# First x tile loaded in halves, the eighth transposed by DMA, and one group of half rows for the last four output tiles

## The chip, the core and the metric

The kernel runs on one core of a Trainium2 chip. The core has five engines that work side by side and wait for each other through semaphores: TensorE (PE; its weight loads are listed apart, as PEld), VectorE (DVE), ScalarE (ACT), GpSimd (POOL) and SyncE (SP), which only issues transfers. ScalarE and GpSimd issue transfers too. Each engine takes its instructions in the order in which they were queued. The metric is the device time of one execution in microseconds (us), the median of several executions.

## The reference

A block with a linear-attention part and a SwiGLU part is run forward, and the gradient with respect to its input and its weights is returned along with the output. There are 2048 rows of 640 columns, in bfloat16.

```
def _layernorm(x, axis=-1, eps=1e-5):
    m = jnp.mean(x, axis=axis, keepdims=True)
    v = jnp.var(x, axis=axis, keepdims=True)
    return (x - m) / jnp.sqrt(v + eps)

...
        qkv = (lambda x, *d: x.transpose(*d))((x @ wqkv).reshape(B, S, 3, H, Dh), 2, 0, 3, 1, 4)
        q, k, v = qkv[0], qkv[1], qkv[2]
        phi = lambda t: jnp.where(t > 0, t + 1, jnp.exp(t)) + 1e-6
        pq, pk = phi(q), phi(k)
        kv = jnp.einsum("bhsd,bhse->bhde", pk, v)
        z = jnp.einsum("bhsd->bhd", pk)
        num = jnp.einsum("bhqd,bhde->bhqe", pq, kv)
        den = jnp.einsum("bhqd,bhd->bhq", pq, z)[..., None] + 1e-6
        o = num / den
        return (lambda x, *d: x.transpose(*d))(o, 0, 2, 1, 3).reshape(B, S, D) @ wo
...
        g = _silu(x @ w_gate)
        u = x @ w_up
        return (g * u) @ w_down

    x = A_x
    h = x + _A_ref(_layernorm(x, axis=-1), A_wqkv, A_wo)
    h2 = h + _B_ref(_layernorm(h, axis=-1), B_w_gate, B_w_up, B_w_down)
    return h2
...
    _out, _vjp = jax.vjp(_f, A_x, A_wqkv, A_wo, B_w_gate, B_w_up, B_w_down)
    _grads = _vjp(grad_out)
```

The outputs are h2 and the gradients of x, wqkv, wo, w_gate, w_up and w_down.

## The kernel before

The 2048 rows are cut into 16 tiles of 128 rows (a row to a partition). In the stages that the change touches, the order of the work is written out by hand: each engine's instructions are queued as the Python code states them, and a library puts a semaphore wait on an instruction whose input or buffer is not free yet.

**The first stage (lines 194 to 400)** computes phi(k) and phi(q) for all 16 tiles. Tile t of x is loaded (load_x, line 201), its mean and variance are taken on VectorE (ln1_stats, L271 and L274), the reciprocal root on GpSimd (ln_rstd, L139 and L140), and x is centred on VectorE: ln1_centre (L278) only subtracts the mean, for the first three tiles, whose scale is applied later; ln1_xn (L282) subtracts and scales. The result must be transposed, 128 columns at a time, before TensorE can multiply it by the weights. For the first XD = 8 tiles TensorE does that: five 128 x 128 transposes into a tile of PSUM, which a copy on VectorE or ScalarE takes to xnT (ln1_tr, ln1_tr1; L289, L296; copies L345, L350). For the other eight tiles a transposing transfer, issued by SyncE, goes straight from xn to xnT (L378). kq_mm (L305) then multiplies the tile by the weights of k and later of q, in ten matmuls of 320 columns each, and ScalarE takes Exp and Relu of the sum (L310, L311); phi adds the two on VectorE, for two tiles at once (L315, L316). The transposes of tile t + 1 stand between the k and the q pass of tile t.

Before the first tile is there, warm (L341) has TensorE multiply an identity matrix by itself 37 times, and 8 times more while ScalarE copies tile 0. The identity is made on GpSimd, and the constants nhalf and ones are set on VectorE. Tile 0 is loaded by a transfer that SyncE issues, tile 1 by one that ScalarE issues; the weights of k follow on SyncE's queue.

SyncE's queue in this stage: the x tiles and weights, then a transposing load of a 448-row piece of w_down (wdT, L255), a transposing load of 512 rows of the output gradient (dh2T, L228), and from there on the transposes of tiles 8 to 15 (L378), with stores of phi(q), phi(k) and xnT to scratch memory (L323, L320, L326) and more pieces of dh2T between them. dh2T and wdT are first used by the stage behind this one (ps_dm, L411, at 61 us).

**PSUM** is handed out as tiles of two banks (512 float32 columns each), from a pool of four: a fifth tile takes over the buffer of the first, and the first writer waits until its last reader is done.

**The last stage (lines 978 to 1063)** computes the output tiles, h plus the SwiGLU part's product with w_down, which has 1728 = 13 x 128 + 64 rows. For each tile and each chunk of its columns, 13 matmuls of full 128 rows and one of the remaining 64 rows are summed in PSUM (part, L1023). The 64-row matmuls are collected: halves_at says after which tile those of several tiles are issued together, alternately on the upper and the lower 64 rows of TensorE's array, so that two run side by side. finish (L1030) adds h on VectorE and stores the tile. The last tile is taken in three chunks, of 320, 192 and 128 columns, that lie in two PSUM tiles by turns; each chunk is added and stored by itself (L1049, L1050). Between the output tiles stand small blocks of weight gradients, dwo and dwv (small_of).

Of the kernel before, what the change touches and what calls it, by code (L numbers as in the profile page):

```python
# [15 lines left out]
P = 128  # L16
# [4 lines left out]
def kernel(  # L21
# [179 lines left out]
    def load_x(eng, t0, t1):  # L201
        return eng.dma_start(out=x_tm[t0 // 8][:, t0 % 8:(t1 - 1) % 8 + 1, :], in_=x_v[:, t0:t1, :])

    load_x(nc.sync, 0, 1)
    load_x(nc.scalar, 1, 2)
    w_k = A_wqkv[:, D:2 * D].rearrange("(k p) n -> p k n", p=P)
    w_q = A_wqkv[:, 0:D].rearrange("(k p) n -> p k n", p=P)
# [29 lines left out]
    with tc.manual_schedule(engines={EngineType.Pool}):  # L237
        ident = const.tile([P, P], BF16, name="ident")
        make_identity(nc, ident[:])
        nhalf = const.tile([P, 4], FP32, name="nhalf")  # L240
        nc.vector.memset(nhalf[:], -0.5)
        ones = const.tile([P, P], BF16, name="ones")
        nc.vector.memset(ones[:], 1.0)
    mask = const.tile([P, 160], BF16, name="mask")
    zb = const.tile([P, D], BF16, name="zb")
    dzb = const.tile([P, D], BF16, name="dzb")
# [15 lines left out]
    pk = big.tile([P, ST, D], BF16, name="pk", tag="B")  # L262
    pqa = big.tile([P, ST, D], BF16, name="pqa", tag="B")
    NC = 3
    XD = 8
    BY_V = (1, 2, 3)

    def ln1_stats(t):
# [14 lines left out]
                                scalar2=rstd1[:, t:t + 1], op0=ALU.subtract, op1=ALU.mult)  # L283

    def ln1_tr(t):
        tp = psum.tile([P, 2, 2 * 512], BF16, name="ps_t", tag="mm")
        for c, (k0, k1) in enumerate(((0, 3), (3, DT))):
            for kt in range(k0, k1):
                nc.tensor.transpose(tp[:, c, (kt - k0) * P:(kt - k0 + 1) * P], xn[:, t, kt * P:(kt + 1) * P], ident[:])  # L289
        return [(slice(k0, k1), tp[:, c, :(k1 - k0) * P].rearrange("p (k c) -> p k c", c=P))  # L290
                for c, (k0, k1) in enumerate(((0, 3), (3, DT)))]

    def ln1_tr1(t):
        tp = psum.tile([P, D], BF16, name="ps_t", tag="mm")
# [40 lines left out]
    with tc.manual_schedule(engines={EngineType.PE, EngineType.DVE, EngineType.Activation, EngineType.Pool, EngineType.SP}):  # L335

        ps = mm("ps_warm")

        def warm(n):
            for _ in range(n):  # L340
                nc.tensor.matmul(ps[:, 0, :P], lhsT=ident[:], rhs=ident[:], start=True, stop=True)  # L341

        def copies(t, eng_copy):
            for sl, src in ln1_tr(t):
                c = eng_copy(out=xnT[:, t, sl], in_=src)  # L345
                if t == 0 and sl.start == 0:
                    wait_for(c, load_3())

        def copy1(t):
            (nc.vector.tensor_copy if t in BY_V else nc.scalar.copy)(out=xnT[:, t], in_=ln1_tr1(t))  # L350

        warm(37)
        ln1_stats(0)
        ln1_centre(0, 0, 3 * P)
        ln1_centre(0, 3 * P, D)
        copies(0, nc.scalar.copy)
        warm(8)
        ln1_stats(1)
        ln1_centre(1)
        kq_mm(0, 0, lambda: copies(1, nc.vector.tensor_copy), PIECES)  # L360
        ln1_stats(2)
        ln1_centre(2)
        kq_mm(1, 0, None, PIECES)
        ln1_stats(3)
        kq_mm(0, 1, lambda: copy1(2), PIECES)
        phi(0, 0)
        ln1_xn(3)
        kq_mm(1, 1)
        for t in range(2, ST):
            if t == 2:  # L370
                ln1_stats(4)
            if t == 4:
                ln1_stats(t + 3)
            if 4 <= t < ST - 4:
                ln1_stats(t + 4)
            if XD <= t + 3 < ST:
                ln1_xn(t + 3)
                nc.sync.dma_start_transpose(out=xnT[:, t + 3], in_=xn[:, t + 3, :])  # L378
            kq_mm(t, 0, (lambda: copy1(t + 1)) if t + 1 < XD else None)
            if t == 2:  # L380
                ln1_stats(5)
            if t == 3:
                ln1_stats(6)
            if t == ST - 1:
                phi(0, t - 1, 1)
            kq_mm(t, 1)
            if t == 3:
                phi(1, 0)
            elif t == ST - 1:
                last_phi = phi(0, t, 1)  # L390
            elif t > 3:
                phi(t % 2, t - 2 - t % 2)
            if t + 2 < XD - 1:
                ln1_xn(t + 2)
            if t == XD - 4:
                ln1_xn(t + 3)
            if ST - NC - 1 <= t < ST - 1:
                ln1_xn(t - ST + NC + 1)
            for f, *a in queue.get(t, ()):
                f(*a)  # L400
# [424 lines left out]
    with tc.manual_schedule(engines={EngineType.SP, EngineType.DVE}):  # L825
# [175 lines left out]
        for t in range(3):  # L1001
            load_h1(t)
        small_of = {2: [(dwo, 0)], 3: [(dwo, 1)], 6: [(dwo, 2), (dwv, 0)], 7: [(dwo, 3), (dwv, 1)],
                    10: [(dwo, 4), (dwv, 2)], 11: [(dwo, 5), (dwv, 3)], 13: [(dwv, 4)]}
        halves_at = {1: range(4), 5: range(4, 8), 9: range(8, 12), 12: (12, 13), 14: (14, 15)}
        pso = {}

        def chunks(t):
            return NCH if t < ST - 1 else [(0, 320), (320, 512), (512, 640)]

        def po(t, ci):
            tile, bank = (0, ci) if t < ST - 1 else (ci % 2, ci // 2)
            if (t, tile) not in pso:
                pso[t, tile] = mm("ps_o")
            n0, n1 = chunks(t)[ci]
            return pso[t, tile][:, bank, :n1 - n0]

        opened = set()

# [7 lines left out]
        def finish(t):  # L1027
            h1r = h1rs.pop(t)
            if t < ST - 1:
                nc.vector.tensor_tensor(out=half(h1r[:]), in0=row(pso.pop((t, 0))), in1=half(h1r[:]), op=ALU.add)  # L1030
                (nc.gpsimd if t < 10 else nc.scalar).dma_start(out=o0_v[:, t, :], in_=h1r[:])
            return h1r

        for t in range(ST):
            if t + MTA < ST:
                load_mT(t + MTA)
            if t < 3:
                for j in (2 * t, 2 * t + 1):
                    tr_cols(Y[:, j, :], scr_Yt, OH[j])
            if t + 3 < ST:  # L1040
                load_h1(t + 3)
            if t == ST - 1:
                h1r = finish(t)
            late = t in (0, 1, 4, 5, 8, 9, 12, 14)
            for ci, (n0, n1) in enumerate(chunks(t)):
                for j in range(FT - 1):
                    part(t, ci, j, None, j == FT - 2 and not late)
                if t == ST - 1:
                    nc.vector.tensor_tensor(out=h1r[:, n0:n1], in0=po(t, ci), in1=h1r[:, n0:n1], op=ALU.add)  # L1049
                    (nc.sync, nc.scalar, nc.sync)[ci].dma_start(out=o0_v[:, t, n0:n1], in_=h1r[:, n0:n1])  # L1050
            if t in halves_at:
                n = 0
                for u in halves_at[t]:
                    for ci in range(len(chunks(u))):
                        part(u, ci, FT - 1, n % 2, u <= t)
                        n += 1
                for u in halves_at[t]:
                    if u <= t:
                        finish(u)
            elif not late and t < ST - 1:  # L1060
                finish(t)
            for f, i in small_of.get(t, ()):
                f(i)
# [30 lines left out]
```

## Time and profile before

| what | us |
|---|---|
| median of 5 runs | 812.17 |
| the five runs | 812.31, 811.95, 822.43, 812.02, 812.17 |
| the profiled execution, its whole time | 812.03 |
| its span, from the first to the last instruction | 810.3 |
| first matmul of the warm-up, first of kq_mm | 1.56, 6.65 |
| start of the last matmul | 807.12 |
| last output landed | 809.18 |

The profile was taken in one execution. The span is what its views cover; 1.7 us of the execution lie around it. A row of the timeline gives start, duration, engine, line, operation, what is written and read, shapes and the number of equal instructions in a row; in brackets stand the engine's idle time before it and what ended that. The duration of a matmul in the rows runs on while the next one has begun, so steps between the starts of matmuls are the better measure of TensorE's pace. A transfer's row (SPq, ACTq) tells how long the issue took; its landing is told apart.

### The profile page before, as it was taken

The numbers are of one execution on the slowest core, as the hardware profiler recorded it, in microseconds if no ns is written. First come the engines' busy times: TensorE is split into PE (matmuls) and PEld (weight loads), VectorE is DVE, ScalarE is ACT, GpSimd is POOL, SyncE is SP. The second block draws the span as 40 slices with busy tenths as digits, with TensorE's granted clock in tenths as the row PEclk, the third lists the DMA queues.
The fourth block names the chain that finished last, engine by engine and source line by source line (L and its number), as shares of the span: only waits on it lengthen the run. The fifth ranks groups of instructions, "written<-read, shape, count | busy, mean of one in ns | idle before, by whom it ended". The sixth has DMA issues, their size and how long they took to land.

```text
span 810.3 us, 13780 instructions
## 1 busy us (share of the span) xinstructions
PE 805.7 (99%) x5436; PEld 518.2 (64%) x5436; DVE 472.7 (58%) x883; ACT 286.0 (35%) x400; POOL 201.4 (25%) x361
## 2 busy tenths in 40 slices
PE   9999999999999999999999999999999999999998
PEld 7776566555555555555666677777777777777676
DVE  7979988880095028810850148999897366631212
ACT  6963531850283035400831122322323133322010
POOL 4600045222422312221224401211221121112330
PEclk9999999999999999999999999999999999999999
DMA  9999899998679967991597767977499869899994
GB/s 244 202 247 282 173 258 227 241 256 183 199 159 217 210 175 189 214 256 54 123 247 149 262 155 210 230 192 173 114 211 182 175 138 171 168 232 231 200 214 127
DMA packets 281904, 159.79 MB, mean 197 GB/s; under 512 B 240220, under 2 KB 267997, under 8 KB 281840
## 3 DMA queue, kind: packets, MB, share of 16 engines
q1 hardware_dynamic: 256912, 83.43, 56.3%
q0 software_dynamic: 18416, 66.95, 26.6%
q10 hardware_dynamic: 6512, 8.54, 3.8%
q8 instruction: 42, 0.69, 0.4%
q14 instruction: 22, 0.18, 0.1%
HBM read 47.68 MB, written 53.66 MB: 125 GB/s over the span
## 4 chain that ended last, share of the span: by engine, by line
PE 99%; POOL 0%; ACT 0%; issue 0%; DVE 0%; POOLq 0%
PE ps_dw L705 22%; PE ps_dhn L109 14%; PE ps_dxn L965 8%; PE ps_o L1023 7%; PE pg L633 7%; PE pu L638 7%; PE ps_kq L305 5%; PE ps_dwqk L888 5%; PE ps_dm L411 5%; PE ps_gt L763 3%; PE ps_dp L109 3%; PE ps_y L502 3%; PE ps_dk L109 3%; PE ps_a L565 3%; PE pdm L411 2%; PE ps_warm L341 1%
## 5 line engine op out<-in xcount | busy, mean ns | idle before, releaser
L109 PE MATMUL ps_dhn<-wgT,cols 128*128 128x320 bf16 x864 | 119.5, 299 | 0.0
L705 PE MATMUL ps_dw<-dd,hn 128*128 128x448 bf16 (+1 forms) x640 | 118.8, 346 | 0.0
L109 PEld LDWEIGHTS <-cols 128*128 128x128 bf16 x864 | 84.5, 98 | 32.9
L705 PEld LDWEIGHTS <-hn 128*128 128x128 bf16 x640 | 62.6, 98 | 54.2
L707 DVE CAST dwev<-ps_dw 128x896 bf16<-128x896 f32 (+3 forms) x12 | 10.9, 907 | 125.3 <-PE ps_dw L705 97.5
L670 POOL DMA_DIRECT2D scr_dT<-stg x64 | 34.6, 541 | 166.4 <-DMA stg<-dd 165.0
L707 ACT CAST dwev<-ps_dw 128x896 bf16<-128x896 f32 (+1 forms) x20 | 17.6, 878 | 162.3 <-PE ps_dw L705 150.6
L147 DVE CUSTOM_DVE_ANT_0 lb_a<-lb_dy,hn 128x640 bf16<-128x640 bf16 x32 | 26.4, 825 | 64.4 <-ACT lb_dy L145 64.4
L633 PE MATMUL pg<-wgu,hnT 128*128 128x448 bf16 (+1 forms) x320 | 63.6, 346 | 0.0
L638 PE MATMUL pu<-wgu,hnT 128*128 128x448 bf16 (+1 forms) x320 | 63.6, 346 | 0.0
L1023 PE MATMUL ps_o<-wd,mT 128*128 128x320 bf16 (+3 forms) x462 | 61.1, 295 | 0.0
L705 PE MATMUL ps_dw<-m_s,dh 128*128 128x448 bf16 (+1 forms) x320 | 60.4, 346 | 0.0
L965 PEld LDWEIGHTS <-ring 128*128 128x128 bf16 x480 | 47.0, 98 | 18.2
L1023 PEld LDWEIGHTS <-mT 128*128 128x128 bf16 (+1 forms) x462 | 41.8, 97 | 17.5 <-issue 2.6
L965 PE MATMUL ps_dxn<-wqkvT,ring 128*128 128x320 bf16 x320 | 51.3, 299 | 0.0
L705 PEld LDWEIGHTS <-dh 128*128 128x128 bf16 x320 | 31.3, 98 | 27.1
L638 PEld LDWEIGHTS <-hnT 128*128 128x128 bf16 x320 | 31.3, 98 | 27.1
L633 PEld LDWEIGHTS <-hnT 128*128 128x128 bf16 x320 | 31.3, 98 | 27.0
L411 PEld LDWEIGHTS <-dh2T 128*128 128x128 bf16 x320 | 31.0, 98 | 25.1
L411 PE MATMUL ps_dm<-wdT,dh2T 128*128 128x448 bf16 (+1 forms) x240 | 46.5, 344 | 0.0
L305 PE MATMUL ps_kq<-wqk,xnT 128*128 128x320 bf16 x320 | 44.9, 299 | 0.1
L1030 DVE TENSOR_TENSOR h1r<-ps_o,h1r 128x640 bf16<-128x640 f32 x15 | 12.1, 822 | 52.6 <-PE ps_o L1023 52.6
(167 smaller groups left out, 1303.9 us busy)
## 6 DMA issues: line engine op xcount, KB each, us to landing
scr_dT<-stg POOLq DMA_DIRECT2D x48, 224.0 KB, 3.4
cols<-scr_dT POOLq DMA_DIRECT2D x6, 1728.0 KB, 8.3
scr_m<-m_s POOLq DMA_DIRECT2D x12, 448.0 KB, 5.1
cols<-scr_dT ACTq DMA_DIRECT2D x2, 1728.0 KB, 10.3
out_dram<-dwev POOLq DMA_DIRECT2D x30, 112.0 KB, 2.7
scr_dT<-stg POOLq DMA_DIRECT2D x16, 192.0 KB, 2.4
scr_pq<-pqa SPq DMA_DIRECT2D x4, 640.0 KB, 4.9
scr_xnT<-xnT SPq DMA_DIRECT2D x4, 640.0 KB, 5.4
```

The lines of the kernel that those rows point to most:

```text
L109: nc.tensor.matmul(ps[:, ci, :320], lhsT=lhs(k), rhs=rhs(k, *NCH[ci]), start=(start and k == 0), stop=(stop and k == n - 1))
L147: nc.vector.tensor_tensor_reduce(out=a[:], in0=dy[:], in1=xhat, scale=1.0, scalar=0.0, op0=ALU.mult, op1=ALU.add, accum_out=sums[:, 1:2])
L305: nc.tensor.matmul(ps[:, ci, :320], lhsT=xnT[:, t, k, :], rhs=wqk[:, k, w0 + n0:w0 + n1], start=(k == 0), stop=(k == DT - 1))
L411: nc.tensor.matmul(ps[:, c, :w], lhsT=dh2T[:, kt, (t + c) * P:(t + c + 1) * P], rhs=wdT[:, kt, o:o + w], start=(kt == 0), stop=(kt == DT - 1))
L633: nc.tensor.matmul(pg[:, c, :w], lhsT=hnT[:, kt, (t + c) * P:(t + c + 1) * P], rhs=wg[:, kt, 0:w], start=(kt == 0), stop=(kt == DT - 1))
L638: nc.tensor.matmul(pu[:, c, :w], lhsT=hnT[:, kt, (t + c) * P:(t + c + 1) * P], rhs=wg[:, kt, w:2 * w], start=(kt == 0), stop=(kt == DT - 1))
L670: nc.gpsimd.dma_start(out=scr_dT[t + c, :, KO[g]:KO[g] + GK[g], :], in_=stg[:, :GK[g], :])
L705: nc.tensor.matmul(ps[:, c, :w], lhsT=lhs(t), rhs=rhs(t), start=(t == 0), stop=(t == ST - 1))
L707: last = copy(out=ev[:, :len(parts), :w], in_=ps[:, :len(parts), :w])
L888: nc.tensor.matmul(ps[:, ci, :320], lhsT=xn_r[:, t, i * P:(i + 1) * P], rhs=dq[t // 8][:, t % 8, n0:n1] if which == 0 else dk[:, t, n0:n1] ...
L965: nc.tensor.matmul(ps[:, ci, :320], lhsT=lhs[:, i, :], rhs=rhs[:, i, n0:n1], start=(k == 0 and i == 0), stop=(k == 2 and i == DT - 1))
L1023: nc.tensor.matmul(po(t, ci), lhsT=mTs[t // 4][r, t % 4, j, :], rhs=wd[r, j, n0:n1], start=(t, ci) not in opened, stop=last)
```

## The change

Five edits:

- Tile 0 of x is loaded by two transfers of 64 rows each, one issued by SyncE and one by ScalarE; tile 1 follows on ScalarE.
- ones is set first on VectorE, and warm multiplies ones instead of the identity, 41 times instead of 37 ahead of tile 0.
- Tile 0's transposes go into two PSUM tiles, and the three transposes of the first piece and its copy are stated ahead of the second piece. Tile 1's go into one PSUM tile, which VectorE copies in two pieces.
- XD is 7: tile 7, the eighth, is transposed by a transfer that SyncE issues in step t = 4 of the loop, ahead of the first load of dh2T. Its centring on VectorE, and that of tile 6, stand ahead of the pair addition of that step.
- In the last stage the 64-row matmuls of tiles 12 to 15 are issued as one group behind tile 13, tile 15's chunks are 512 and 128 columns in one PSUM tile, its stores go by ScalarE and SyncE, and the block dwv 4 moves from behind tile 13 to behind tile 14.

```diff
--- before.py
+++ after.py
@@ -201,7 +201,8 @@
     def load_x(eng, t0, t1):
         return eng.dma_start(out=x_tm[t0 // 8][:, t0 % 8:(t1 - 1) % 8 + 1, :], in_=x_v[:, t0:t1, :])
 
-    load_x(nc.sync, 0, 1)
+    for eng, p0 in ((nc.sync, 0), (nc.scalar, P // 2)):
+        eng.dma_start(out=x_tm[0][p0:p0 + P // 2, 0, :], in_=x_v[p0:p0 + P // 2, 0, :])
     load_x(nc.scalar, 1, 2)
     w_k = A_wqkv[:, D:2 * D].rearrange("(k p) n -> p k n", p=P)
     w_q = A_wqkv[:, 0:D].rearrange("(k p) n -> p k n", p=P)
@@ -237,10 +238,10 @@
     with tc.manual_schedule(engines={EngineType.Pool}):
         ident = const.tile([P, P], BF16, name="ident")
         make_identity(nc, ident[:])
+        ones = const.tile([P, P], BF16, name="ones")
+        nc.vector.memset(ones[:], 1.0)
         nhalf = const.tile([P, 4], FP32, name="nhalf")
         nc.vector.memset(nhalf[:], -0.5)
-        ones = const.tile([P, P], BF16, name="ones")
-        nc.vector.memset(ones[:], 1.0)
     mask = const.tile([P, 160], BF16, name="mask")
     zb = const.tile([P, D], BF16, name="zb")
     dzb = const.tile([P, D], BF16, name="dzb")
@@ -262,7 +263,7 @@
     pk = big.tile([P, ST, D], BF16, name="pk", tag="B")
     pqa = big.tile([P, ST, D], BF16, name="pqa", tag="B")
     NC = 3
-    XD = 8
+    XD = 7
     BY_V = (1, 2, 3)
 
     def ln1_stats(t):
@@ -283,12 +284,11 @@
                                 scalar2=rstd1[:, t:t + 1], op0=ALU.subtract, op1=ALU.mult)
 
     def ln1_tr(t):
-        tp = psum.tile([P, 2, 2 * 512], BF16, name="ps_t", tag="mm")
-        for c, (k0, k1) in enumerate(((0, 3), (3, DT))):
+        for k0, k1 in PIECES:
+            tp = psum.tile([P, (k1 - k0) * P], BF16, name="ps_t", tag="mm")
             for kt in range(k0, k1):
-                nc.tensor.transpose(tp[:, c, (kt - k0) * P:(kt - k0 + 1) * P], xn[:, t, kt * P:(kt + 1) * P], ident[:])
-        return [(slice(k0, k1), tp[:, c, :(k1 - k0) * P].rearrange("p (k c) -> p k c", c=P))
-                for c, (k0, k1) in enumerate(((0, 3), (3, DT)))]
+                nc.tensor.transpose(tp[:, (kt - k0) * P:(kt - k0 + 1) * P], xn[:, t, kt * P:(kt + 1) * P], ident[:])
+            yield slice(k0, k1), tp[:].rearrange("p (k c) -> p k c", c=P)
 
     def ln1_tr1(t):
         tp = psum.tile([P, D], BF16, name="ps_t", tag="mm")
@@ -338,7 +338,7 @@
 
         def warm(n):
             for _ in range(n):
-                nc.tensor.matmul(ps[:, 0, :P], lhsT=ident[:], rhs=ident[:], start=True, stop=True)
+                nc.tensor.matmul(ps[:, 0, :P], lhsT=ones[:], rhs=ones[:], start=True, stop=True)
 
         def copies(t, eng_copy):
             for sl, src in ln1_tr(t):
@@ -346,10 +346,15 @@
                 if t == 0 and sl.start == 0:
                     wait_for(c, load_3())
 
+        def copy_1():
+            src = ln1_tr1(1)
+            for k0, k1 in PIECES:
+                nc.vector.tensor_copy(out=xnT[:, 1, k0:k1], in_=src[:, k0:k1])
+
         def copy1(t):
             (nc.vector.tensor_copy if t in BY_V else nc.scalar.copy)(out=xnT[:, t], in_=ln1_tr1(t))
 
-        warm(37)
+        warm(41)
         ln1_stats(0)
         ln1_centre(0, 0, 3 * P)
         ln1_centre(0, 3 * P, D)
@@ -357,7 +362,7 @@
         warm(8)
         ln1_stats(1)
         ln1_centre(1)
-        kq_mm(0, 0, lambda: copies(1, nc.vector.tensor_copy), PIECES)
+        kq_mm(0, 0, copy_1, PIECES)
         ln1_stats(2)
         ln1_centre(2)
         kq_mm(1, 0, None, PIECES)
@@ -376,6 +381,8 @@
             if XD <= t + 3 < ST:
                 ln1_xn(t + 3)
                 nc.sync.dma_start_transpose(out=xnT[:, t + 3], in_=xn[:, t + 3, :])
+            if t == XD - 3:
+                ln1_xn(t + 2)
             kq_mm(t, 0, (lambda: copy1(t + 1)) if t + 1 < XD else None)
             if t == 2:
                 ln1_stats(5)
@@ -392,8 +399,6 @@
                 phi(t % 2, t - 2 - t % 2)
             if t + 2 < XD - 1:
                 ln1_xn(t + 2)
-            if t == XD - 4:
-                ln1_xn(t + 3)
             if ST - NC - 1 <= t < ST - 1:
                 ln1_xn(t - ST + NC + 1)
             for f, *a in queue.get(t, ()):
@@ -1001,19 +1006,18 @@
         for t in range(3):
             load_h1(t)
         small_of = {2: [(dwo, 0)], 3: [(dwo, 1)], 6: [(dwo, 2), (dwv, 0)], 7: [(dwo, 3), (dwv, 1)],
-                    10: [(dwo, 4), (dwv, 2)], 11: [(dwo, 5), (dwv, 3)], 13: [(dwv, 4)]}
-        halves_at = {1: range(4), 5: range(4, 8), 9: range(8, 12), 12: (12, 13), 14: (14, 15)}
+                    10: [(dwo, 4), (dwv, 2)], 11: [(dwo, 5), (dwv, 3)], 14: [(dwv, 4)]}
+        halves_at = {1: range(4), 5: range(4, 8), 9: range(8, 12), 13: range(12, 16)}
         pso = {}
 
         def chunks(t):
-            return NCH if t < ST - 1 else [(0, 320), (320, 512), (512, 640)]
+            return NCH if t < ST - 1 else [(0, 512), (512, 640)]
 
         def po(t, ci):
-            tile, bank = (0, ci) if t < ST - 1 else (ci % 2, ci // 2)
-            if (t, tile) not in pso:
-                pso[t, tile] = mm("ps_o")
+            if t not in pso:
+                pso[t] = mm("ps_o")
             n0, n1 = chunks(t)[ci]
-            return pso[t, tile][:, bank, :n1 - n0]
+            return pso[t][:, ci, :n1 - n0]
 
         opened = set()
 
@@ -1027,7 +1031,7 @@
         def finish(t):
             h1r = h1rs.pop(t)
             if t < ST - 1:
-                nc.vector.tensor_tensor(out=half(h1r[:]), in0=row(pso.pop((t, 0))), in1=half(h1r[:]), op=ALU.add)
+                nc.vector.tensor_tensor(out=half(h1r[:]), in0=row(pso.pop(t)), in1=half(h1r[:]), op=ALU.add)
                 (nc.gpsimd if t < 10 else nc.scalar).dma_start(out=o0_v[:, t, :], in_=h1r[:])
             return h1r
 
@@ -1041,13 +1045,13 @@
                 load_h1(t + 3)
             if t == ST - 1:
                 h1r = finish(t)
-            late = t in (0, 1, 4, 5, 8, 9, 12, 14)
+            late = t % 4 < 2
             for ci, (n0, n1) in enumerate(chunks(t)):
                 for j in range(FT - 1):
                     part(t, ci, j, None, j == FT - 2 and not late)
                 if t == ST - 1:
                     nc.vector.tensor_tensor(out=h1r[:, n0:n1], in0=po(t, ci), in1=h1r[:, n0:n1], op=ALU.add)
-                    (nc.sync, nc.scalar, nc.sync)[ci].dma_start(out=o0_v[:, t, n0:n1], in_=h1r[:, n0:n1])
+                    (nc.scalar, nc.sync)[ci].dma_start(out=o0_v[:, t, n0:n1], in_=h1r[:, n0:n1])
             if t in halves_at:
                 n = 0
                 for u in halves_at[t]:
```

## The prediction, made before the changed kernel was run

> **What bounds the kernel now.** I read the page first: how busy is each engine, and what is the chain that ended last made of?
>
> ```profile
> PE 805.7 (99%) x5436; PEld 518.2 (64%) x5436; DVE 472.7 (58%) x883; ACT 286.0 (35%) x400; POOL 201.4 (25%) x361
> ...
> PE 99%; POOL 0%; ACT 0%; issue 0%; DVE 0%; POOLq 0%
> ```
>
> TensorE is the chain. A 99% busy row may hide slow stretches, so I went through the matmul starts one by one: a 320-column matmul follows the last after 0.136 us, a 128-column one after 0.056. From 6.65 us to the last start at 807.12 no step is over 0.1 us longer than its width explains. So only three things count: when the first real matmul starts, how much TensorE work there is, and what follows the last matmul. A new wait of TensorE counts in full.
>
> The head, from the timeline (start, duration, engine, line; in brackets the idle time before and what ended it):
>
> ```profile
> 0.93 0.17 DVE L243 MEMSET ones<- 128x128 bf16 x1
> ...
> 1.55 3.87 PEld L341 LDWEIGHTS <-ident 128*128 128x128 bf16 x37 [1.55 <-POOL ident masks.py:199]
> ...
> 3.96 0.89 DVE L271 BATCH_NORM_STATS2 st<-x_tm 128x6 f32<-128x320 bf16 x2 [2.87 <-DMA x_tm<-in_A_x_dram]
> ...
> 5.50 0.57 PE L289 MATMUL ps_t<-ident,xn 128*128 128x128 bf16 x5
> ...
> 6.11 0.75 ACT L345 COPY xnT<-ps_t 128x384 bf16<-128x384 bf16 x2 [3.61 <-PE ps_t L289]
> ...
> 6.64 0.66 PEld L305 LDWEIGHTS <-xnT 128*128 128x128 bf16 x6 [0.30 <-ACT xnT L345]
> ```
>
> The 37 warm matmuls and tile 0's transposes meet at 5.50: one ends as the other's data is there. The copy starts at 6.11, when all five transposes are out (the fifth ends at 6.075, the third at 5.964). The clock column reads 1.00 throughout, but 128-column steps are 0.107 us until about 5.75 and 0.056 after: in the rows, TensorE speeds up 4.2 us after its first matmul.
>
> SyncE's queue where the new transpose goes, and the tail:
>
> ```profile
> 9.73 8.11 SPq L255 DMA_TRANSPOSE wdT<-in_B_w_down_dram  x1
> 17.89 3.28 SPq L228 DMA_TRANSPOSE dh2T<-in_grad_out_dram  x1
> 24.50 1.20 SPq L378 DMA_TRANSPOSE xnT<-xn  x1
> ```
>
> ```profile
> 805.64 0.49 DVE L1049 TENSOR_TENSOR h1r<-ps_o,h1r 128x320 bf16<-128x320 f32 x1 [1.29 <-PE ps_o L1023]
> 806.15 1.89 SPq L1050 DMA_DIRECT2D out_dram<-h1r  x2
> 806.65 0.36 DVE L1049 TENSOR_TENSOR h1r<-ps_o,h1r 128x192 bf16<-128x192 f32 x1 [0.53 <-PE ps_o L1023]
> 807.04 0.34 ACTq L1050 DMA_DIRECT2D out_dram<-h1r  x1
> 807.38 0.29 DVE L1049 TENSOR_TENSOR h1r<-ps_o,h1r 128x128 bf16<-128x128 f32 x1 [0.37 <-PE ps_o L1023]
> ```
>
> SyncE sits free from 21.17 to 24.50, then issues almost without a pause. In the tail the first add ends at 806.13, before the 128-column chunk begins at 806.45.
>
> **Part 1, the head.** Tile 0 landed at 3.94 us, sharing the rings with tile 1 (landed 3.77). In halves it lands between 3.94 (no gain) and about 3.1 (half of ScalarE's 128 packets were out by 2.5 us, all by 3.3: 0.8 earlier); I take 3.5. That buys little, because TensorE is in order and the warm matmuls stand ahead of the transposes. `ones` is ready at about 1.04 (its memset now first, at 0.87, for 0.17), so TensorE starts at 1.10 instead of 1.56; four more matmuls at 0.107 give 0.43 of the 0.46 back. Transposes start at 5.47: -0.03. With two PSUM tiles the copy is released by the third transpose: 6.075 - 5.964 = -0.11. Sum -0.14 if the speed-up stays at 5.75; if it comes 4.2 us after the first matmul, at 5.30, the last two warm matmuls and three transposes take 0.056 instead of 0.107, up to another 0.2: -0.34. Ends: 0 (tile 0 as late as now and the 41 too long) and -0.34; I take the middle, -0.24. Tile 1 goes behind a half on ScalarE's queue (0.3 later, needed at about 5.1, landed at 3.8); its one-tile copy on VectorE already waits for all five transposes today (7.95 against 7.92): both cost nothing, and 0.1 at most without that cover.
>
> The Trainium skill ("TensorE: Matmul & The Clock Gate", Part 1) says the gate opens on a free-running 3.4 us window, not after a count of matmuls. By it the earlier start is worth nothing certain, and executions would differ by up to a window, some 1.7 us at half speed; the head would be -0.14 with that scatter. Four of the five runs lie within 0.36 us, which speaks against so large a scatter here.
>
> **Part 2, tile 7 by DMA.** TensorE loses five transposes: tile 6's k pass with them takes 24.715 to 26.353 = 1.638 us, tile 7's without 27.711 to 29.069 = 1.358. Gain 0.28. ScalarE loses a 0.69 us copy, off the path. VectorE has tile 7's and tile 6's centring ahead of the pair addition instead of behind it: tile 6's is earlier, the addition 0.8 later, and its readers (a store; a buffer reused two tiles on, 3 us later) have room. On SyncE the transpose waits for tile 7's centring, which needs GpSimd's rstd of 21.09: issue at about 21.6, where today the 512-row load of dh2T went at 17.89. Behind it: that load (first used after 60 us) ends its issue at 21.6 + 1.20 + 3.28 = 26.1 and tile 8's transpose goes then, 1.6 later than 24.50. Tile 7 lands at 24.5 to 25.9 (rows of this line: 2.85 to 4.3 us to landing), needed at 27.4. Tile 8 lands at 29.0 to 30.4; needed at 30.43 today, and 30.43 - 0.28 - 0.24 = 29.9 then. Tiles 9 to 12 had 1.6 to 2.2 us in hand and keep some 0.5. I take 0, as a short DMA queue (the dh2T rows have moved by then) is nearer to 2.85; the other end is 0.5.
>
> **Part 3, one group for the last four tiles.** Each change between whole and half rows costs 0.09 us twice. From the last whole matmul to the next, less its own 0.136: the group of four took 0.473, of five 0.526, the group of eight at 782.6 took 0.746. The new group is one of eight whose last pair is 512 wide instead of 320 (+0.08): 0.83 instead of 1.00, -0.17. Tile 12's add and store move behind tile 13: two adds of 0.82 beside 3.5 us of matmuls, nothing. The moved weight-gradient block (0.30 of TensorE either way) has its copy (0.69) and store (1.9 to landing) done by about 807 on ScalarE, ahead of the last chunk's store there.
>
> **Part 4, the last tile in one PSUM tile.** 13 x (0.136 + 0.0825 + 0.056) = 3.57 becomes 13 x (0.216 + 0.056) = 3.53: -0.04. But in the built program the first 128-column matmul now waits for VectorE's count of the 512-column add. The wait goes by tile, not by bank: as in the head, where a copy of one bank waited for the other bank's transposes. In the kernel before, a chunk in the other tile lies between. Price: the add starts 0.39 us after the last matmul of a 320-wide chunk starts (805.242, 805.636), 0.47 for 512 (0.08 longer). Adds take 0.29, 0.36, 0.49, 0.82 for 128, 192, 320, 640 columns, so 0.69 for 512. TensorE resumes about 0.055 later (today's step from a copy's end to 8.363). Sum 1.21, less the 0.216 it would have taken anyhow: +1.00. Queued behind are 13 matmuls, the last add (0.29) and the last store (1.48 to landing), which decide the end. The 128 KB store by ScalarE lands some 0.3 us before that one and costs at most 0.1.
>
> The Trainium skill ("PSUM — Partial Sum Buffer", PSUM bank collisions) asks for guards by bank and quadrant; the chunks lie in two banks. By that rule alone the wait is needless and the tail would be -0.21, the sum 811.4. The program's semaphores decide, and they do wait.
>
> **Sum.** The profiled execution took 812.03 (span 810.3, 1.7 around it). 812.03 - 0.24 - 0.28 - 0.17 - 0.04 + 1.00 = 812.30. The median of the runs is 0.14 above the profiled execution: 812.44.
>
> **The rivals.**
> - *The wait in the tail is free* (its semaphore has long counted, or the add is far shorter): 812.44 - 1.0 = 811.4. For it: all other parts are gains. Against it: the count waited for is that of the add itself. Chance 0.12.
> - *SyncE's queue becomes the bound, slower.* It decides as soon as tile 8 lands after 29.9. With the row's slower 4.3 us to landing it is 30.4: +0.5, 812.9. With the longest issues seen, 2.0 for a transpose and 5.35 for a 512-row load (at 62.3 us, under heavy traffic): 21.6 + 2.0 + 5.35 + 4.3 = 33.3, +3.4, 815.8. For it: SyncE issues without pause from 24.5, so a delay is hardly made up. Against it: the rings are empty from 22.6 to 25.4 now. Chance 0.2, nearly all of it near 812.9.
> - *The speed-up comes later*, half a window and more: +0.5 to +1.7, 813 to 814. Against it: the small scatter. Chance 0.05.
> - *The halves do nothing* (tile 0 is no earlier): 0.1 to 0.24 lost, 812.6; inside the forecast, whose chance is 0.63.
>
> **How the numbers follow.** Forecast 812.4. Downwards the first rival sets 811.4, upwards the second 812.9 with the head's gain lost 813.1; 811.4 to 813.2 leaves out the long ends of the second and third rival. About 1%, 8.1 us, is what a measurement of this kernel can tell from no change; no case reaches it. Only an unseen stall could: 0.02 slower, 0.01 faster, 0.97 within.
>
> **What would show it.** In the changed profile: the warm weight loads from 1.1 us; the copy of tile 0 while its last two transposes run; the first real weight load at 6.3 to 6.5; in the tail a matmul gap of about 1.0 us released by VectorE between the 512- and the 128-column chunk, the last add 0.8 us later against the start of tile 12. A gap in the matmuls between 27 and 42 us would mean SyncE's queue; no gap in the tail, that the wait was misread.

## The result: 2.9 us slower, and the profile after

The changed kernel takes 815.08 us (median of 50 runs) where the kernel before takes 812.19 (94 runs beside them): the ratio of the two is 1.0037, with a 95% interval from 1.0026 to 1.0047. The prediction was 812.4, with a range up to 813.2. The profiled execution took 815.08 with a span of 813.4, against 812.03 and 810.3 before.

I read the page in the same order as before: the busy times and the chain that ended last.

```profile
PE 806.6 (99%) x5421; PEld 517.5 (64%) x5421; DVE 472.6 (58%) x882; ACT 285.7 (35%) x399; POOL 200.9 (25%) x361
...
PE 95%; DVE 3%; DMA 1%; issue 0%; ACTq 0%; DVEq 0%
```

TensorE's busy time grew by only 0.9 us, with 15 matmuls fewer. But where TensorE had been 99% of the chain it is now 95%, and VectorE and a DMA have come in: TensorE waits for others. So I went through the matmul starts again and listed each step that is longer than the matmul's width explains. Before, there was none over 0.1 us after 6.65 us. Now there are five of consequence.

The head, in the timeline (start, duration, engine, line, operation; in brackets the idle time before and what ended it):

```profile
1.11 4.29 PEld L341 LDWEIGHTS <-ones 128*128 128x128 bf16 x41 [1.11 <-DVE nhalf L244]
...
1.41 0.85 ACTq L202 DMA_DIRECT2D x_tm<-in_A_x_dram  x1
...
3.62 0.89 DVE L272 BATCH_NORM_STATS2 st<-x_tm 128x6 f32<-128x320 bf16 x2 [2.55 <-DMA x_tm<-in_A_x_dram]
...
5.46 0.74 PE L290 MATMUL ps_t<-ident,xn 128*128 128x128 bf16 x5
...
6.03 0.75 ACT L345 COPY xnT<-ps_t 128x384 bf16<-128x384 bf16 x2 [2.45 <-PE ps_t L290]
6.35 0.89 DVE L272 BATCH_NORM_STATS2 st<-x_tm 128x6 f32<-128x320 bf16 x2 [1.05 <-DMA x_tm<-in_A_x_dram]
...
6.66 0.70 PEld L305 LDWEIGHTS <-xnT 128*128 128x128 bf16 x6
...
7.96 0.45 PE L296 MATMUL ps_t<-ident,xn 128*128 128x128 bf16 x5 [0.27 <-DVE xn L279]
```

The first half of this is as predicted: the warm matmuls start at 1.11, tile 0 reaches VectorE at 3.62 instead of 3.96, the copy starts while the last two transposes still run. Yet the first product starts at 6.71, not earlier than the 6.65 of before: the fall of a 128-column step from 0.107 to 0.056 us came at 6.57 here, and the transposes ran slow. And tile 1, issued by ScalarE at 1.41, reaches VectorE only at 6.35. Before, its transfer had landed at 3.77, and VectorE took it up as soon as it was done with tile 0:

```profile
5.56 0.88 DVE L271 BATCH_NORM_STATS2 st<-x_tm 128x6 f32<-128x320 bf16 x2
```

Now tile 1's transposes wait until 7.96: 0.43 us of TensorE.

SyncE's queue, and what TensorE's weight loads waited for in the same stretch:

```profile
22.09 1.20 SPq L383 DMA_TRANSPOSE xnT<-xn  x1
23.34 2.86 SPq L229 DMA_TRANSPOSE dh2T<-in_grad_out_dram  x1
26.30 1.22 SPq L383 DMA_TRANSPOSE xnT<-xn  x1
...
31.81 1.89 SPq L383 DMA_TRANSPOSE xnT<-xn  x1
```

```profile
36.77 5.28 PEld L305 LDWEIGHTS <-xnT 128*128 128x128 bf16 x40 [0.86 <-DMA xnT<-xn]
42.38 2.56 PEld L305 LDWEIGHTS <-xnT 128*128 128x128 bf16 x20 [0.34 <-DMA xnT<-xn]
46.35 1.75 PEld L305 LDWEIGHTS <-xnT 128*128 128x128 bf16 x14 [1.41 <-DMA xnT<-xn]
```

Tile 7's transpose goes out at 22.09, the load of dh2T behind it, tile 8's transpose at 26.30 (24.50 before) and tile 10's at 31.81. Before, that one stood here:

```profile
29.86 1.80 SPq L378 DMA_TRANSPOSE xnT<-xn  x1
```

TensorE then waits for tiles 10, 12 and 13. By the matmul starts these gaps are 0.69, 0.17 and 1.24 us, 2.10 together.

The tail:

```profile
808.84 0.69 DVE L1053 TENSOR_TENSOR h1r<-ps_o,h1r 128x512 bf16<-128x512 f32 x1 [2.33 <-PE ps_o L1027]
809.56 0.34 ACTq L1054 DMA_DIRECT2D out_dram<-h1r  x1
809.58 0.89 PE L1027 MATMUL ps_o<-wd,mT 128*128 128x128 bf16 x13 [0.84 <-DVE h1r L1053]
```

The 128-column matmuls start when the 512-column add is over; the gap by the matmul starts is 1.00.

At the last matmul's start the trace of after is 3.12 us behind (810.24 against 807.12). The parts: first product +0.06, tile 1 +0.43, the three gaps +2.10, five transposes fewer -0.28, the wait in the tail +1.00, and one group of half rows with the last tile's wider chunks -0.23 (from the switch back to whole rows after tile 11 to the last start: 23.63 before, 24.40 after, less the 1.00). Sum 3.08. So the loss has three places: SyncE's queue, the tail, tile 1.

Three of the profiles below (the changed kernel with tile 0 whole, the kernel before with halves, and the one with the load ahead) were taken in executions with a wait of 4.6 to 5.5 us near 757 us that, by their times, most executions of the same kernels do not have; of these only the first 100 us are used.

### The profile page after: what moved, and what is told of

Same layout as the page of the kernel before. It is cut to its first block, busy times and chain, and to the rows that moved or that the text cites. A ratio compares the mean times of both kernels' runs of the same rounds, so it can differ in the third digit from the quotient of the medians.

```text
span 813.4 us, 13751 instructions
## 1 busy us (share of the span) xinstructions
PE 806.6 (99%) x5421; PEld 517.5 (64%) x5421; DVE 472.6 (58%) x882; ACT 285.7 (35%) x399; POOL 200.9 (25%) x361
## 4 chain that ended last, share of the span: by engine, by line
PE 95%; DVE 3%; DMA 1%; issue 0%; ACTq 0%; DVEq 0%
PE ps_dw L710 22%; PE ps_dhn L109 14%; PE ps_dxn L970 8%; PE ps_o L1027 7%; PE pu L643 7%; PE pg L638 7%; PE ps_dwqk L893 5%; PE ps_dm L416 5%; PE ps_dk L109 3%; PE ps_gt L768 3%; PE ps_dp L109 3%; PE ps_y L507 3%; PE ps_a L570 3%; PE pdm L416 2%; PE ps_kq L305 2%; DVE st L272 1%
## 5 line engine op out<-in xcount | busy, mean ns | idle before, releaser
L712 ACT CAST dwev<-ps_dw 128x896 bf16<-128x896 f32 (+1 forms) x20 | 17.6, 879 | 161.9 <-PE ps_dw L710 139.3
```

What stands on the lines that cost most here:

```text
L712: last = copy(out=ev[:, :len(parts), :w], in_=ps[:, :len(parts), :w])
```

## The experiments

Each run was timed beside the kernel before, whose median was 812.2 each time. The ratio of a run's time to that of the kernel before has an interval of 0.1 to 0.3% to either side, 0.7 to 2.7 us, which is wider than most effects here. So the verdicts rest on TensorE's gaps in the profile, of which there is one for each kernel, and the medians (given as the difference from the kernel before, timed beside it; the changed kernel has +2.89) only stand beside them.

### Undoing one part of the changed kernel

**The last stage as before.** Groups, three chunks in two PSUM tiles, place of the weight-gradient block.

```diff
-        halves_at = {1: range(4), 5: range(4, 8), 9: range(8, 12), 13: range(12, 16)}
+        halves_at = {1: range(4), 5: range(4, 8), 9: range(8, 12), 12: (12, 13), 14: (14, 15)}
-            return NCH if t < ST - 1 else [(0, 512), (512, 640)]
+            return NCH if t < ST - 1 else [(0, 320), (320, 512), (512, 640)]
...
-            if t not in pso:
-                pso[t] = mm("ps_o")
+            tile, bank = (0, ci) if t < ST - 1 else (ci % 2, ci // 2)
+            if (t, tile) not in pso:
+                pso[t, tile] = mm("ps_o")
```

> The changed kernel with the last stage wholly as before (groups of half rows, three chunks of the last tile in two PSUM tiles, place of the weight-gradient block). Theory (the wait between the 512- and the 128-column chunk is only a third of the loss, SyncE's queue costs twice as much): the 1.00 us gap in the tail goes, the group's 0.21 is given back, so 0.8 below the changed kernel, about 814.3 against 812.2 before: +2.1 remains. Rival (the loss is the tail wait, and the gaps in the first stage are made up later): equal to before within 0.3. The three gaps of matmuls at 36 to 47 us stay under both.

+2.01: 0.88 better than the changed kernel. The tail's gap is gone, from the switch after tile 11 to the last start it takes 23.63 us as before, and the gaps before tiles 10 and 12 stay (1.29 and 0.30). The theory holds: the tail is under a third of the loss.

**Only the wait taken away.** Two chunks as in the change, in a PSUM tile each, and the groups and the place of the weight-gradient block of before.

```diff
-            if t not in pso:
-                pso[t] = mm("ps_o")
+            tile, bank = (0, ci) if t < ST - 1 else (ci, 0)
+            if (t, tile) not in pso:
+                pso[t, tile] = mm("ps_o")
```

> The changed kernel with the last tile's 512- and 128-column chunk in a PSUM tile each, which takes the wait between them away, and for that with the groups of half rows as before (pairs 12,13 and 14,15; the freed PSUM tile has to come from somewhere). Theory (the wait is by PSUM tile and costs 1.00): the gap before the first 128-column matmul goes, the two extra switches between whole and half rows give 0.17 back, 0.8 below the changed kernel, and 0.0 to 0.1 below the run with the whole last stage as before. Rival (the wait covers something, the last add or the store of 512 columns, that then is late itself): the last store lands no earlier and the gain is under 0.3. The gaps at 36 to 47 us stay.

+2.44, only 0.45 better. TensorE gains what was expected: from the switch after tile 11 to the last start it takes 23.63 us instead of 24.40. But in VectorE's timeline the two last adds now stand back to back:

```profile
809.17 0.96 DVE L1054 TENSOR_TENSOR h1r<-ps_o,h1r 128x512 bf16<-128x512 f32 x2 [2.35 <-PE ps_o L1028]
```

The 128-column add waits for the 512-column add (0.69) instead of for TensorE, and from the last matmul's start to the end of the span it is 3.33 us instead of 3.13. So 0.20 of the wait covered something, as the rival had it, and 0.58 is what the profile gains. The expectation that this run ends 0.0 to 0.1 below the one with the whole last stage as before failed: its median is 0.41 above it (814.62 and 814.21), and in the profiles the end behind the last matmul's start is 0.27 longer (3.33 and 3.06). The wait itself goes by PSUM tile: the two chunks lay in two banks in the changed kernel too, and only with a tile each does it vanish.

**The load of dh2T ahead of tile 7's transpose on SyncE.**

```diff
-    queue = {4: [(load_dh2T, 0)], 5: [(store_q, 0)], ...
+    queue = {3: [(load_dh2T, 0)], 5: [(store_q, 0)], ...
```

> The changed kernel with the first 512-row load of dh2T issued one step earlier, ahead of tile 7's transpose on SyncE's queue. Theory (order of SyncE's issues): the load goes out in the idle stretch from 17.4 us, tile 7's transpose at about 22, tile 8's at about 24, so tiles 8 to 14 land at least 1.5 us earlier; the gaps of 0.69, 0.17 and 1.24 us at 36 to 47 us vanish and the time is 2.1 below the changed kernel, about 813.0. Rival (one more transposing transfer takes ring time that the later ones lack, wherever it stands): the gaps stay at 1 us or more in sum, and the gain is under 1. A second risk: tile 7 itself is needed at 27.4 and now stands behind a 3.3 us issue that starts at 17.4; it should land by 26.

+1.80, 1.09 better, between the two expectations: the load goes out at 15.73, but gaps of 0.59 (tile 10) and 1.09 (tile 13) stay. Tile 8's centring ended at 25.08, so its transpose went at 25.11, and its issue took 2.62 instead of 1.22 us (a fetch of 16 KB of instructions ran from 25.92 to 27.34, in the middle of it). Tile 10 went at 31.07. So the order alone did not put it right here, and neither theory was enough.

**Tile 0 whole, tile 1 first on ScalarE's queue.**

```diff
-    for eng, p0 in ((nc.sync, 0), (nc.scalar, P // 2)):
-        eng.dma_start(out=x_tm[0][p0:p0 + P // 2, 0, :], in_=x_v[p0:p0 + P // 2, 0, :])
+    load_x(nc.sync, 0, 1)
```

> The changed kernel with tile 0 loaded whole by SyncE and tile 1 first on ScalarE's queue again; all else as changed. Theory (the second place on ScalarE's queue makes tile 1 land at 6.3 instead of 3.8, which makes the 0.43 us gap of TensorE at 7.4 us): tile 1 lands before 4.2 and the gap goes; tile 0 lands at 3.9 instead of 3.6, so VectorE is up to 0.3 later with tile 0's centring, which the warm matmuls (until 5.46) hide or not. Time 0.1 to 0.5 below the changed kernel. Rival (the gap comes from VectorE's order, not from the transfer): the gap stays at 0.3 or more with tile 1 landed by 4.2. The instant at which the 128-column step falls from 0.107 to 0.056 us is read as well: if it comes 4.2 to 5.5 us after the first matmul in no fixed way, it does not belong to the change.

+2.40, 0.49 better. Tile 1 lands at 4.02 and the gap at 7.4 is gone. The gaps before tiles 10 and 13 stay (0.92 and 1.40), 2.32 together instead of 2.10: TensorE, less delayed at the head, waits 0.22 more for SyncE. So the gain of 0.43 is not kept whole as long as SyncE is late.

**All three together.**

> The three undone together: last stage as before, dh2T's load ahead of tile 7's transpose, tile 0 whole. What is left of the change is tile 7 by DMA (0.28 of TensorE), the earlier warm matmuls and the two PSUM tiles of tile 0 (0.1 to 0.3). Theory (the three are all of the loss): 0.3 to 0.6 below the kernel before, 811.6 to 811.9. Rival (tile 7 by DMA costs something of its own): at or above 812.2.

+0.14, 2.75 better than the changed kernel. No gap is left before 700 us: tile 8's transpose goes at 24.72 with an issue of 1.20, tile 10's at 30.15. Within the noise (the ratio to the kernel before lies from 0.996 to 1.003) what the three parts cost is all of the loss. The gain of 0.3 to 0.6 on the kernel before did not show in the median (12 runs from 811.25 up), which is where the rival put it. But the profiled execution, 812.98, has a wait of 1.21 us at 755.25, before the same block of dwo as the longer waits named above, that the profiles of before and of the changed kernel do not have; without it, it would stand at 811.8. Whether tile 7 costs something of its own was thus left open here. That the first-stage gaps vanish only with two edits together left open whether the order on SyncE causes them at all, so I went to the kernel before and made the parts one by one.

### One part of the change in the kernel before

**Tile 7 by DMA, nothing else** (`XD = 7`, with the order of centring that the change has).

> The kernel before with one edit: tile 7 by DMA, with the order of centring that goes with it. Theory (SyncE's queue, with the load of dh2T behind tile 7's transpose, is by itself late enough): gaps before tiles 10 and 13 of 1.5 to 2.3 us in sum, less 0.28 of transposes: 1.3 to 2.0 above before, about 813.8. Rival (the queue only fails together with TensorE's 0.43 us delay by tile 1, as putting either right in the changed kernel left most of the gaps): no gap, 0.28 below before, 811.9. TensorE starts at 1.56 on the identity as before: when its step falls to 0.056 us says whether the later fall of 6.3 to 6.8 us seen in five profiles with the earlier start (5.80 in the one of before) goes with that start.

+1.10, with one gap of 1.11 us before tile 10; the load of dh2T is issued at 23.17, tile 8's transpose at 26.06, tile 10's at 31.70. Tile 13 lands at 44.70, in time. So tile 7 by DMA makes SyncE late by itself, without the late tile 1; only the size was less than expected. The fall of the 128-column step came at 7.1 us here, with the first matmul at 1.56, so a late fall does not need the earlier start.

**The same with the load of dh2T one step earlier** (the edit shown above).

> The kernel before with tile 7 by DMA, and the load of dh2T one step earlier, ahead of tile 7's transpose: against the run with tile 7 by DMA alone it changes nothing but the order of two issues on SyncE. Theory (the order is the cause; one more transposing transfer costs nothing by itself): the load is issued at about 17.4 and out by 21, tile 7 at about 21.7, tile 8 by 24.8 with an issue of 1.2; no gap before tile 10 or 13, and 0.28 below before apart from the instant of the speed-up. Rival (the extra transfer): a gap of 0.5 or more stays.

-0.32 (811.86; the interval of the ratio, 0.997 to 1.003, does not exclude no gain). SyncE's timeline:

```profile
17.61 3.03 SPq L228 DMA_TRANSPOSE dh2T<-in_grad_out_dram  x1
21.57 5.17 SPq L378 DMA_TRANSPOSE xnT<-xn  x2
26.84 0.54 SPq L323 DMA_DIRECT2D scr_pq<-pqa  x1
27.46 1.82 SPq L378 DMA_TRANSPOSE xnT<-xn  x1
29.33 0.57 SPq L326 DMA_DIRECT2D scr_xnT<-xnT  x1
30.00 1.89 SPq L378 DMA_TRANSPOSE xnT<-xn  x1
```

The load lies in the idle stretch from 17.6 again, tiles 7 and 8 follow (21.57 and 24.61), tile 10 goes at 30.00, and TensorE has no gap in the stage. From the first product to the first matmul of the next stage it takes 45.23 us, where before it took 45.51: that is the 0.28 of the five transposes. The same transfers in another order: the extra transposing transfer costs nothing.

**The load of dh2T one step later, tile 7 left on TensorE.**

```diff
-    queue = {4: [(load_dh2T, 0)], 5: [(store_q, 0)], ...
+    queue = {5: [(load_dh2T, 0), (store_q, 0)], ...
```

> The kernel before, tile 7 still transposed by TensorE, with only the load of dh2T moved one step later, behind tile 8's transpose on SyncE and ahead of the store of q. Theory (order alone): tile 8 as before (24.5), the load 25.7 to 29.0, so tile 9 is issued at about 30.3 instead of 27.2 and lands at about 34 against 33.1 needed; with the 16 KB instruction fetch near 43 the gaps are 1.5 to 4 in sum, and the time is that much above before. Rival (it takes the extra transposing transfer to make SyncE late): no gap over 0.3, time as before.

+2.79. The load is issued from 25.58 to 29.31, tile 9's transpose at 30.04, and TensorE waits:

```profile
34.28 2.56 PEld L305 LDWEIGHTS <-xnT 128*128 128x128 bf16 x20 [1.47 <-DMA xnT<-xn]
37.34 7.99 PEld L305 LDWEIGHTS <-xnT 128*128 128x128 bf16 x60 [0.51 <-DMA xnT<-xn]
46.42 1.61 PEld L305 LDWEIGHTS <-xnT 128*128 128x128 bf16 x13 [1.08 <-DMA xnT<-xn]
```

By the matmul starts 1.30, 0.34 and 0.91, 2.55 together. The order alone makes the loss, with no change to any tile. Across all profiles one number sorts the kernels, the instant at which SyncE issues tile 10's transpose:

| kernel | tile 10 issued | landed | tile 13 landed | gaps in the stage |
|---|---|---|---|---|
| before | 29.86 | 34.02 | 41.85 | 0 |
| before, tile 7 by DMA, load ahead | 30.00 | 34.59 | 42.27 | 0 |
| before, halves, tile 1 by SyncE | 30.02 | 35.32 | 43.20 | 0 |
| before, new head without halves | 30.09 | 35.43 | 42.57 | 0 |
| changed, three parts put right | 30.15 | 34.54 | 42.23 | 0 |
| before, halves | 30.38 | 34.95 | 42.24 | 0 |
| changed, load ahead | 31.07 | 36.59 | 45.84 | 1.68 |
| changed, two PSUM tiles at the end | 31.48 | 36.76 | 46.30 | 2.34 |
| changed, tile 0 whole | 31.60 | 36.60 | 46.17 | 2.32 |
| before, tile 7 by DMA | 31.70 | 36.97 | 44.70 | 1.11 |
| changed | 31.81 | 36.73 | 46.30 | 2.10 |
| changed, last stage as before | 31.82 | 37.34 | 45.53 | 1.59 |
| before, load one step later | 32.62 | 37.30 | 46.38 | 2.55 |

Up to 30.4 nothing is lost, from 31.1 on 1 to 2.6 us; each row is one profile. That is why two edits had to come together to rid the changed kernel of the gaps: alone, each moved the queue by 0.2 or 0.7 us, which did not bring it from 31.81 to 30.4.

**Tile 0 in halves, nothing else.**

> The kernel before with one edit: x tile 0 loaded in halves of 64 partitions by SyncE and ScalarE, so tile 1 is second on ScalarE's queue. Theory: tile 1 lands near 6.3 us, TensorE has a gap of 0.4 to 0.6 at 7.4; tile 8's transpose is issued some 0.4 later, with the load of dh2T already out, so no gap or a small one at 36 to 47: +0.4 to +0.6 on before, 812.7. Rival A (tile 1 late by itself is enough to make SyncE's queue late): +1.5 or more. Rival B (the late landing of tile 1 is an accident of the other edits): no gap, time as before.

+0.36. Tile 1 lands at 6.30, TensorE's gap is 0.38, and there is none later. The mechanism of the theory holds; gap and time are just under their ranges.

**Halves, with tile 1 second on SyncE's queue instead of ScalarE's.**

```diff
-    load_x(nc.scalar, 1, 2)
+    load_x(nc.sync, 1, 2)
```

> The kernel before with x tile 0 in halves of 64 partitions, and tile 1 second on SyncE's queue ahead of the weights instead of second on ScalarE's. Theory (halves land no earlier than the whole: the later one at 3.6 to 4.0 in five profiles, the whole at 3.7 to 3.9; what they cost is tile 1's place behind the weights): tile 1 lands by 5, no gap at 7.4; the first weights land some 0.5 later, at most 0.2 of which reaches the first product; time within 0.3 of before. Rival (ScalarE's or SyncE's second issue is what is slow): tile 1 lands at 6 or later and the gap stays at 0.35 or more.

+0.14. Tile 1 is issued at the same instant and lands at 3.93; no gap at 7.4:

```profile
1.43 0.56 SPq L202 DMA_DIRECT2D x_tm<-in_A_x_dram  x1
2.04 0.43 SPq L209 DMA_DIRECT2D wqk<-in_A_wqkv_dram  x1
...
5.05 0.88 DVE L272 BATCH_NORM_STATS2 st<-x_tm 128x6 f32<-128x320 bf16 x2
```

So it is not the second place on a queue that made it late. In the changed kernel ScalarE's issue of tile 1 took 0.85 us and ended at 2.26, while SyncE's first weight load had ended its issue at 1.98 and its second followed at 2.51. Tile 1's packets with data moved only from 4.46 us on (4.1 to 4.5 in the five profiles with this order), when 259 of the weights' 640 had moved, and the rest of the weights moved among them. Issued by SyncE ahead of the weights, it landed before most of them. That it was the weights and not ScalarE's longer issue is argued from these instants: this run changed both the engine and the place.

**The new head without the halves.**

> The kernel before with the head of the changed one except the halves: ones first, 41 warm matmuls on it from 1.11 us, tile 0 in two PSUM tiles and its second copy released early, tile 1 in one PSUM tile. Theory 1 (the speed-up comes in a window that does not follow the first matmul): the fall of the step to 0.056 comes anywhere from 5 to 8.5 us; the time is 0.1 below to 0.6 above before and scatters. Theory 2 (the earlier start by itself shifts the fall to 6.3 to 6.8 us, as in all five profiles with it): +0.0 to +0.2, with as little scatter as before. Theory 3 (as predicted): -0.14 to -0.34.

+0.08, no gap. The gain of theory 3 did not come; theories 1 and 2 both allow this run. The fall of the step, from 0.107 to 0.056 us for 128 columns, came at 6.9 us, 5.8 after the first matmul, and the first product started at 6.85.

## Why the prediction was wrong, by its steps

**Part 2 failed.** The mechanism was named, as the second rival, and the step that threw it out was this: "Tiles 9 to 12 had 1.6 to 2.2 us in hand and keep some 0.5. I take 0, as a short DMA queue (the dh2T rows have moved by then) is nearer to 2.85; the other end is 0.5." The margins were right (before, tile 10 landed at 34.02 and was used at 35.86), but the delay was looked at for tile 8 alone and taken to stay there. Tile 8 itself cost nothing partly by luck: it landed at 30.26, later than the 29.9 at which the forecast needed it, but TensorE, late by the head, came to it only at 30.65. The delay grew with the tiles: against before, tile 8 landed 1.47 us later, tile 9 2.19, tile 10 2.70, tile 13 4.45.

SyncE issues without a pause from 22 us, so the 1.8 us at tile 8 were never made up, and the stores and loads between the transposes carried them on; then the transfers themselves took longer, 4.92 us from issue to landing for tile 10 (4.17 before) and 4.85 for tile 13 (2.85 before). Tile 13's longer transfer goes with something in the trace: a fetch of 16 KB of instructions runs from 43.73 to 45.23 in the changed kernel's trace, and from 44.8 to 46.0 the queues' packets hardly move. The DMA view of 44.5 to 46.0 us, in 40 slices (the transfer engines' busy share in tenths, and what they moved):

```profile
DMA  9999999900000000000100001001001001000000
GB/s 184 184 191 164 82 55 48 20 0 0 0 0 0 0 0 0 0 0 0 14 7 7 7 7 14 7 7 14 7 7 14 7 7 14 7 14 7 7 14 7
```

Before, tile 13 had landed at 41.85, ahead of that fetch (it begins at 42.80 there); now its transfer lies across it. The other profiles sort the same way: in the five where the fetch begins 2.0 us or more ahead of the landing tile 13 took 4.44 to 5.15 us, in the two where it begins 0.2 us ahead 3.57 and 3.69, and in the six where it begins as tile 13 lands or later 2.85 to 3.58. No run moved the fetch alone, so that it holds the transfer up is not shown. Why tile 10's transfer is longer is open.

The price of the step: 2.10 in the changed kernel, 1.11 alone, 0 to 0.5 forecast. The gain of 0.28 stands in the profile of the run with the load ahead (45.23 instead of 45.51 us for the stage); its median, -0.32, agrees but does not settle it.

**Part 1 failed in both its terms.** The first is "Tile 1 goes behind a half on ScalarE's queue (0.3 later, needed at about 5.1, landed at 3.8)", which was to cost nothing. It landed 2.56 later, at 6.33: I counted the queue that tile 1 was on and not the weight loads on the other queue, whose issue now ended ahead of it. Price 0.43. The second is the gain of 0.24, which was to come from an earlier tile 0 and an earlier start. Tile 0 is hardly earlier: in six profiles with halves the later half lands at 3.76 us on average (3.44 to 4.03), in seven with the whole tile it lands at 3.84 (3.68 to 4.00). The Trainium skill ("DMA: Bandwidth & Descriptors", Issuing engines are not separate DMA queues) says that issuing from several engines saves only the time of issue; these averages agree, and here even the issue was no shorter (0.57 us for 64 rows, 0.40 for 128).

The earlier start brought nothing: the first product came at 6.68 us on average in the seven profiles with the first matmul at 1.11, and at 6.61 in the six with 1.56. The speed-up does not follow the first matmul at a fixed distance. It came 2.8 to 5.8 us after it in thirteen profiles, and at 4.4 to 7.1 us of the span. (Six of the seven with the earlier start lie at 6.3 to 6.9, the seventh at 4.8; whether the start moves it on average is open.) In the changed kernel it came 0.8 later than before, as the rival "the speed-up comes later" had it, but the first product came 0.30 later than forecast and not 0.5 or more. I had discounted the page of the skill that says so, "TensorE: Matmul & The Clock Gate", Part 1, by the small scatter of five runs. It speaks of a free-running window of 3.4 us, and the spread of 3.0 us fits within one. The same section has the instant vary by 500 ns to either side only, and in these profiles it varies by three times that. The scatter in time is smaller than the window because an early speed-up only shortens the warm matmuls: TensorE then waits for tile 0 (0.42 and 0.39 us before the first transpose, where the step fell at 4.8, and 0.48 where it fell at 4.4), and only what is late of the speed-up reaches real work. The first product started between 6.34 and 6.87 us in all profiles.

The 0.11 that the two PSUM tiles were to give came to the copy and not to the product. In the changed kernel the copy's first piece was done at 6.51 (6.59 before), but of the eight warm matmuls behind the transposes five still ran at 0.107 us, and they kept TensorE until 6.71. Where the step had fallen at 4.8, the first product came 0.91 us after the first transpose with the two tiles (the run without the wait in the tail) and 1.05 without them (the kernel before with the load ahead).

**Part 3 and Part 4 were right.** The group and the wider chunks gave 0.23 where 0.21 was put down, the wait cost 1.00 as put down (of which 0.20 came back in the last add when it was taken away). The rival "the wait in the tail is free" is refuted by the gap and by the run that takes it away. That the program's wait goes by tile and not by bank, argued in the prediction, is shown.

So the sum had the right sign and missed 2.1 us in one term and 0.7 in another (0.43, and +0.06 in place of -0.24). With these terms as measured it is 812.44 + 2.10 + 0.73 = 815.27, against 815.08.

## What to carry to other kernels

A transfer that goes ahead in an engine's queue delays everything behind it until that engine has an idle stretch: follow each later consumer's margin down to that stretch, with the slowest landing that the trace shows, and don't stop at the first. Look for the idle stretch that the old order used (here 17.4 to 22 us) and keep a long issue in it. And when a load changes its place, compare where its issue ends with every other queue's, not only with its own.

## What the runs showed of the hardware that was not expected

- Two loads were issued at the same instant, 1.41 and 1.42 us, by two engines. The one whose issue ended 0.28 us later had its first packet of data at 4.46, behind 259 packets of the other queue, and landed at 6.33. In the run that issued it ahead of that queue's loads it landed at 3.93.
- A load of 64 partitions by 640 took 0.57 us to issue, of 128 partitions 0.40.
- Fetches of 16 KB of instructions (0.9 to 1.6 us each) stand in all thirteen traces of this stage; one begins between 25.4 and 27.7 us, another between 42.8 and 45.3. An issue of SyncE that ran during the first took longer: 2.62 instead of 1.22 for a transpose in the changed kernel with the load ahead, 1.44 instead of 0.53 for the store of q in the changed kernel. Around the second the queues' packets stood nearly still for about 1 us: from 44.8 to 46.0 in the changed kernel, from 43.0 to 44.0 before. That the fetch is the cause is not shown.
- The step of a 128-column matmul of TensorE first fell from 0.107 to 0.056 us at 4.8 to 6.9 us of the span with the first matmul at 1.11, and at 4.4 to 7.1 with it at 1.56.
